# Leaving one branch of a nonlinearity out of the common path, with a check at the end and a recomputation behind a branch

## The chip, the cores and the metric

The kernel runs on one core of a Trainium2 chip. The metric is the device time of one execution in microseconds (us); the kernel before has a median of 1015.11 us in three runs (1015.0 to 1015.22).

## The reference

Three parts follow one another. A linear attention over q, k and v of (4, 8, 576, 64) gives 2304 tokens of 512 numbers. A first layer with a nonlinearity of its own takes them through 2048 hidden columns. A second layer sends each token to two of eight experts.

```python
def _moe_ref(x, w_in, w_out) -> np.ndarray:
    h = x @ w_in
    g = h - np.tanh(h)
    return (g @ w_out).astype(np.float32)
...
    noisy_logits = logits + noise_scale * noise
    top2 = np.argpartition(-noisy_logits, 2, axis=1)[:, :2]
...
            h = np.maximum(x[mask] @ w1[e], 0.0)
            out[mask] += top2_w[mask, k, None] * (h @ w2[e])
```

w_in and w_out arrive as 64-bit floats, and the kernel decodes them on the chip from their two 32-bit halves. With the reference's inputs h is small: its largest magnitude is 0.017.

## The kernel before

All matrix products of the two layers are made of three products of split operands: each operand is the sum of a rounded high part and the rest, and high x high, high x rest and rest x high are added in PSUM (L814 to L816 for the first product of a layer, L874 to L876 for the second).

The work of both layers is a list of units, `seq`. A unit of the first layer is one block of 384 tokens (six blocks, 0 to 5) and one of 16 slices of 128 hidden columns: `l1` computes h into one of two PSUM banks, `nonlin` computes the negative of g, `split` makes its high part on ScalarE and its rest on GpSimd (L861), and `l2` multiplies it with w_out three units later (`LAG`). Blocks 0 and 1 run interleaved, since they need each decoded weight slice first; blocks 2 to 5 follow one after the other. While blocks 0 and 1 run, `decode` turns the 16 slices of w_in and w_out into split weights: three bit operations on VectorE (L712, L713, L717) for each half slice, a rounding on ScalarE (L722) and a subtraction on GpSimd (L724). The next slices are loaded in SP's queue (`raw_load`, tiles `stage` and `raw`), which waits for a free buffer; behind them in the same queue stand the fills of the buffer `xs` and of the output with zeros and the loads of q, k and v for later blocks.

`nonlin` has two branches for h. Where h squared is at most 0.09 (`HC` is 0.3), a polynomial in u = h*h is used: p = -u*h * ((sqrt(G_Q)*(u + G_A))**2 + G_B). Elsewhere tanh(h) - h is taken. Both are computed for every element:

```python
        a1 = A.activation(tu, h, AF.Square)
        a2 = A.activation(tt, h, AF.Tanh)
        a3 = A.activation(tq, tu, AF.Square, bias=qbias[:, 0:1], scale=math.sqrt(G_Q))
        a4 = A.activation(tm, tu, AF.Relu, bias=qbias[:, 1:2])
...
        v4 = V.copy_predicated(tp, tm.bitcast(U32), tt)
```

Four instructions run on ScalarE and four on VectorE: L839 (-u*h), L840 (tanh(h) - h), L845 (times the polynomial) and L846 (the choice). For a few units a table `KN` moves the work of L845 to GpSimd (L843). The bank of h is free for the next unit but one when its last reader, L840, is through.

After the first layer, `route_*` compute each token's two experts, `scatter` writes the tokens to areas of `xs`, one per expert, with 608 rows computed in any case, and the units of the second layer read them from there. `overflow_counts` counts the rows of each expert during the second layer. At the end, `overflow` holds a branch: an expert with more rows than 608 gets the rest computed there. In the profiled execution that branch is not taken.

The order of the instructions on each engine is set by a scheduler from priorities, `issue_after` marks and the offsets in `KN`; `hooks` tie the steps to units.

Of the kernel before, what the change touches and what calls it, by code (L numbers as in the profile page):

```python
# [375 lines left out]
def moe_kernel(ctx, tc, q, k, v, w_in, w_out, w_gate, w_noise, noise, w1, w2, out, xs):  # L376
# [150 lines left out]
    gap = cp.tile([P, GAPS], F32, name="gap")  # L527
    prow = cp.tile([P, 1], F32, name="prow")
# [163 lines left out]

    W = {}
# [126 lines left out]
    def nonlin(U):  # L820
# [10 lines left out]
        tt = sp.tile([P, n], F32, tag="t", bufs=8, name=f"t{U}")  # L831
        tm = sp.tile([P, n], F32, tag="t", bufs=8, name=f"m{U}")
# [129 lines left out]
    def route_slots(blk):  # L962
# [15 lines left out]
        if blk == NBLK - 1:  # L978
# [19 lines left out]
    def scatter(blk, t):  # L998
        xa, sl = XA[blk], SL[blk]
        for i in range(2):  # L1000
            G.memset(spacer, 0.0)
            st = G.indirect_dma_start(out=xs, out_offset=bass.IndirectOffsetOnAxis(ap=sl[:, i, t:t + 1], axis=0),
                                      in_=xa[:, t, :], in_offset=None)
            for o in last_scatter:
                tc.declare_no_dep(st.ins, o.ins, reason="every token has its own rows")
            last_scatter.append(st)

    tiles_x = cp.tile([P, E + 1], I32, name="tiles_x")
    pad_row = cp.tile([P, E], I32, name="pad_row")

    def overflow_counts():
# [4 lines left out]
        V.tensor_add(c[:, 0, 0:GAPS], c[:, 0, 0:GAPS], gap)  # L1016
        V.tensor_add(c[:, 1, :], c[:, 0, :], eoff[:, 0, :])
        V.tensor_scalar(pad_row, c[:, 1, :], prow, None, op0=OP.add)
        V.tensor_scalar(c[:, 2, :], c[:, 0, :], float(P - 1 - CAP), 0.0, op0=OP.add, op1=OP.max)
        V.tensor_copy(tiles_x[:, 0:E], c[:, 2, :])  # L1020
        V.tensor_scalar(tiles_x[:, 0:E], tiles_x[:, 0:E], 7, None, op0=OP.logical_shift_right)
# [4 lines left out]
    def overflow():  # L1026
# [3 lines left out]
        with tc.If(some > 0):  # L1030
# [3 lines left out]
            for e in range(E):  # L1034
# [7 lines left out]
                with tc.For_i(0, n, 1) as it:  # L1042
# [6 lines left out]
                    for c in range(NC):  # L1049
                        T.transpose(pt[:, c * P:(c + 1) * P], x[:, c * P:(c + 1) * P], ident)  # L1050
# [173 lines left out]
```

## Time and profile before

| | us |
|---|---|
| median of three runs | 1015.11 |
| the profiled execution | 1017.24 |
| its span, first to last instruction | 1015.4 |
| TensorE busy | 958.9 (94%) |
| VectorE busy | 627.2 (62%) |
| ScalarE busy | 455.8 (45%) |
| GpSimd busy | 285.5 (28%) |

The span is divided below into stretches: up to 48 us the attention of block 0 and the first loads, 48 to 178 us blocks 0 and 1 with the decode, 178 to 500 us the rest of the first layer up to the middle of block 5, 500 to 580 us the change to the second layer, then the experts, and from 1005.5 us the last scatter. In the profile PE is TensorE, DVE VectorE, ACT ScalarE, POOL GpSimd, SP the queue engine. A row of a wait names who waited, for whom, the sum in us, how often, and the longest. A row of a line gives the busy time and the mean length of one instruction in ns. Busy time is the union of the rows, so rows of one engine can add up to a little more.

### The profile page before, as it was taken

The numbers are of one execution on the slowest core, as the hardware profiler recorded it, in microseconds if no ns is written. First come the engines' busy times: TensorE is split into PE (matmuls) and PEld (weight loads), VectorE is DVE, ScalarE is ACT, GpSimd is POOL, SyncE is SP. The second block draws the span as 40 slices with busy tenths as digits, with TensorE's granted clock in tenths as the row PEclk, the third lists the DMA queues.
The fourth block names the chain that finished last, engine by engine and source line by source line (L and its number), as shares of the span: only waits on it lengthen the run. The fifth ranks groups of instructions, "written<-read, shape, count | busy, mean of one in ns | idle before, by whom it ended". The sixth has DMA issues, their size and how long they took to land.

```text
span 1015.4 us, 14696 instructions
## 1 busy us (share of the span) xinstructions
PE 958.9 (94%) x5311; PEld 844.0 (83%) x5311; DVE 627.2 (62%) x1339; ACT 455.8 (45%) x981; POOL 285.5 (28%) x278
## 2 busy tenths in 40 slices
PE   4988887999999999999989999999999999999996
PEld 2766676989888999999978888988889888888885
DVE  7999999876778856756774623635353534444221
ACT  2665564676556556566754312423232323333110
POOL 4555546422234242242241211111101011111102
PEclk9999999999999999999999999999999999999999
DMA  9935775111342010010350641845353645443203
GB/s 260 334 114 171 240 282 182 39 40 26 74 130 77 25 65 22 21 65 1 104 177 30 209 100 23 216 112 137 79 174 62 167 100 131 106 113 79 27 12 49
DMA packets 106962, 111.13 MB, mean 109 GB/s; under 512 B 28032, under 2 KB 79232, under 8 KB 106880
## 3 DMA queue, kind: packets, MB, share of 16 engines
q1 hardware_dynamic: 98496, 90.40, 28.8%
q0 software_dynamic: 8384, 19.70, 10.2%
q8 instruction: 44, 0.72, 0.3%
q14 instruction: 38, 0.31, 0.1%
HBM read 74.87 MB, written 35.21 MB: 108 GB/s over the span
## 4 chain that ended last, share of the span: by engine, by line
PE 74%; DVE 13%; DMA 5%; issue 4%; POOL 2%; ACT 1%; SPq 1%; DVEq 0%; POOLq 0%; ACTq 0%
PE y L876 11%; PE y L875 11%; PE y L874 11%; PE h L814 11%; PE h L816 11%; PE h L815 11%; DVE dec L713 2%; DMA stage<-in_moe_w_in 2%; DVE p L845 2%; PE xgt L782 1%; DVE p L846 1%; DVE dec L717 1%; PE lg L912 1%; DMA xg<-xs 1%; PE xp L688 1%
## 5 line engine op out<-in xcount | busy, mean ns | idle before, releaser
L876 PE MATMUL y<-w,g 128*128 128x512 f32 (+1 forms) x608 | 240.6, 396 | 0.2
L875 PE MATMUL y<-w,g 128*128 128x512 f32 (+1 forms) x608 | 240.4, 395 | 0.0
L874 PE MATMUL y<-w,g 128*128 128x512 f32 (+1 forms) x608 | 240.2, 395 | 0.0
L826 ACT ACTIVATE g<-h 128x352 fp32r<-128x352 f32 (+1 forms) x128 | 54.3, 424 | 315.2 <-PE y L876 307.4
L827 DVE SCALAR_TENSOR_TENSOR g<-h,g 128x352 fp32r<-128x352 f32 (+1 forms) x128 | 60.5, 472 | 217.7 <-ACT g L826 217.7
L861 POOL TENSOR_TENSOR g<-p,g 128x384 fp32r<-128x384 f32 x96 | 104.4, 1089 | 224.5 <-ACT g L860 79.9
L1075 POOL DMA_INDIRECT out<-yo,gm x40 | 62.8, 1569 | 364.6 <-DVE yo L1074 266.8
L814 PE MATMUL h<-xgT,w 128*128 128x352 f32 (+1 forms) x512 | 159.5, 311 | 0.6 <-DVE g L827 0.6
L814 PE MATMUL h<-xT,w 128*128 128x384 f32 x384 | 135.8, 355 | 24.3 <-DVE t L840 15.9
L815 PE MATMUL h<-xgT,w 128*128 128x352 f32 (+1 forms) x512 | 154.4, 302 | 1.2 <-DVE xgT L784 1.2
L816 PE MATMUL h<-xgT,w 128*128 128x352 f32 (+1 forms) x512 | 154.4, 302 | 0.0
L876 PEld LDWEIGHTS y<-w,g 128*128 128x128 f32 (+1 forms) x608 | 112.5, 185 | 30.0 <-POOL g L861 1.4
L816 PE MATMUL h<-xT,w 128*128 128x384 f32 x384 | 131.0, 341 | 0.5 <-POOL w L724 0.5
L815 PE MATMUL h<-xT,w 128*128 128x384 f32 x384 | 130.4, 340 | 1.0 <-DVE xT L691 1.0
L875 PEld LDWEIGHTS y<-w,g 128*128 128x128 f32 (+1 forms) x608 | 112.6, 185 | 19.0
L874 PEld LDWEIGHTS y<-w,g 128*128 128x128 f32 (+1 forms) x608 | 112.7, 185 | 17.7 <-ACT g L860 0.2
L814 PEld LDWEIGHTS h<-xT,w 128*128 128x128 f32 x384 | 73.1, 191 | 33.8 <-DVE t L840 19.7
L814 PEld LDWEIGHTS h<-xgT,w 128*128 128x128 f32 x512 | 96.5, 188 | 5.3 <-DVE g L827 1.2
L815 PEld LDWEIGHTS h<-xgT,w 128*128 128x128 f32 x512 | 96.7, 189 | 4.8 <-DVE xgT L784 1.6
L816 PEld LDWEIGHTS h<-xgT,w 128*128 128x128 f32 x512 | 96.4, 188 | 0.0
L839 DVE SCALAR_TENSOR_TENSOR p<-u,h 128x384 f32<-128x384 f32 x96 | 52.7, 549 | 58.7 <-ACT t L835 54.2
L744 DVE TENSOR_TENSOR w<-raw,w 128x512 fp32r<-128x512 f32 x128 | 84.3, 694 | 6.5 <-ACT w L742 5.6
(181 smaller groups left out, 1465.1 us busy)
## 6 DMA issues: line engine op xcount, KB each, us to landing
raw<-in_moe_w SPq DMA_DIRECT2D x128, 256.0 KB, 3.2
xs<-pad SPq DMA_DIRECT2D x16, 528.0 KB, 6.6
xg<-xs SPq DMA_DIRECT2D x16, 528.0 KB, 4.3
stage<-in_moe_w_in SPq DMA_DIRECT2D x13, 512.0 KB, 10.0
stage<-in_moe_w_out SPq DMA_DIRECT2D x13, 512.0 KB, 9.7
out<-pad SPq DMA_DIRECT2D x4, 1280.0 KB, 8.9
qr<-in_q SPq DMA_DIRECT2D x20, 192.0 KB, 3.5
k<-in_k SPq DMA_DIRECT2D x8, 256.0 KB, 5.7
```

Source lines behind the costliest of these rows:

```text
L744: V.tensor_sub(wt[:, 2 * i + 1, :], s, wt[:, 2 * i, :].bitcast(F32))
L814: T.matmul(h, wh, x[:, 0, c, :], start=(c == 0), stop=False)
L815: T.matmul(h, wh, x[:, 1, c, :], start=False, stop=False)
L816: T.matmul(h, wl, x[:, 0, c, :], start=False, stop=(c == NC - 1))
L826: LA[U] = A.activation(g[:, 0, :], h, AF.Relu)
L827: LV[U] = V.scalar_tensor_tensor(g[:, 1, :], h, 0.0, g[:, 0, :].bitcast(F32), op0=OP.max, op1=OP.subtract)
L839: v1 = V.scalar_tensor_tensor(tp, tu, -1.0, h, op0=OP.mult, op1=OP.mult)
L861: G.tensor_sub(g[:, 1, :], tp, g[:, 0, :].bitcast(F32))
L874: T.matmul(y, gh, w[:, 2, :], start=first, stop=False)
L875: T.matmul(y, gh, w[:, 3, :], start=False, stop=False)
L876: T.matmul(y, gl, w[:, 2, :], start=False, stop=last)
L1075: o = G.indirect_dma_start(out=out, out_offset=bass.IndirectOffsetOnAxis(ap=g.bitcast(U32)[0:m, t, 1:2], axis=0), in_=yo[0:m], in_offset=N ...
```

## The change

`nonlin` keeps the polynomial branch alone. Tanh, the mask, the subtraction L840 and the choice L846 go; the square of h also adds up its values per partition into a column of a new tile `usum`, one column per unit. All units compute the last product on VectorE, and GpSimd's L843 goes. For the check at the end the largest of the 96 sums of each partition is compared with 0.09, and a matmul with ones counts the partitions above. The sum over 384 tokens is at least its largest member, so no single square above 0.09 passes unseen. The final branch, now `rare`, is taken if an expert overflows or if the count is above zero; in the second case `general` clears the output, loads and decodes the weights again, computes the first layer with both branches and routes and computes all experts anew. For that the split inputs of the six blocks are saved to a new buffer `xd` in HBM (`x_save`), 1536 KB each.

```diff
-        a1 = A.activation(tu, h, AF.Square)
-        a2 = A.activation(tt, h, AF.Tanh)
-        a3 = A.activation(tq, tu, AF.Square, bias=qbias[:, 0:1], scale=math.sqrt(G_Q))
-        a4 = A.activation(tm, tu, AF.Relu, bias=qbias[:, 1:2])
-        ACTS[U] = (a1, a2, a3, a4)
+        a1 = A.activation(tu, h, AF.Square, accum_out=usum[:, U:U + 1])
+        a2 = A.activation(tq, tu, AF.Square, bias=qbias[:, 0:1], scale=math.sqrt(G_Q))
+        ACTS[U] = (a1, a1, a2, a2)
         v1 = V.scalar_tensor_tensor(tp, tu, -1.0, h, op0=OP.mult, op1=OP.mult)
-        v3 = V.tensor_sub(tt, tt, h)
-        if K('tqp%d' % U, 0):
-            A.activation(tq, tq, AF.Relu, bias=qbias[:, 2:3])
-            v2 = PS[U] = G.tensor_mul(tp, tp, tq)
-        else:
-            v2 = V.scalar_tensor_tensor(tp, tq, G_B, tp, op0=OP.add, op1=OP.mult)
-        v4 = V.copy_predicated(tp, tm.bitcast(U32), tt)
-        VS[U] = (v1, v3, v3 if U in PS else v2, v4)
-        LA[U], LV[U] = a4, v4
+        v2 = V.scalar_tensor_tensor(tp, tq, G_B, tp, op0=OP.add, op1=OP.mult)
+        VS[U] = (v1, v1, v2, v2)
+        LA[U], LV[U] = a2, v2
...
+    def x_save(blk):
+        Y.dma_start(xd[blk], XT[blk].bitcast(F32).rearrange("p a c s -> p (a c s)"))
...
+        V.tensor_reduce(over, usum, axis=AX, op=OP.max)
+        V.tensor_scalar(over_b, over, HC * HC, None, op0=OP.is_gt)
+        T.matmul(pp[:, E:E + 1], ones_b, over_b, start=True, stop=True)
+        V.tensor_copy(tiles_x[:, E + 1:E + 2], pp[:, E:E + 1])
         V.tensor_reduce(c[:, 1, 0:1], c[:, 0, :], axis=AX, op=OP.add)
+        V.tensor_add(c[:, 1, 0:1], c[:, 1, 0:1], pp[:, E:E + 1])
         V.tensor_copy(tiles_x[:, E:E + 1], c[:, 1, 0:1])
...
+    def rare():
+        some = nc.values_load(tiles_x[0:1, E:E + 1], min_val=0, max_val=E * (AREA // P) + P,
                               skip_runtime_bounds_check_because=why)
         with tc.If(some > 0):
...
+            expert_rows(CAP)
+            big = nc.values_load(tiles_x[0:1, E + 1:E + 2], min_val=0, max_val=P,
+                                 skip_runtime_bounds_check_because=why)
+            with tc.If(big > 0):
+                general()
...
+    for blk in range(NBLK):
+        at(pos["m", 0, 5] + blk if blk < 2 else pos["m", blk, 2], x_save, blk)
```

The line numbers shift: L814 to L816 become L818 to L820, L839 keeps its number, L845 becomes L840, L712, L713 and L717 become L716, L717 and L721, and the maximum of q, L654, becomes L655.

VectorE at the decode of column 10, before: u, q, t, m and p are the tiles of `nonlin`, `dec` those of a decode; `stage_466` is column 9, `stage_683` column 10.

```order
L839 SCALAR_TENSOR_TENSOR p_1077<-u_1073,h_1059 128x384
L717 SCALAR_TENSOR_TENSOR dec_1_1052<-stage_466,dec_1_1052 128x512
L840 TENSOR_TENSOR t_1075<-t_1075,h_1059 128x384
L845 SCALAR_TENSOR_TENSOR p_1077<-q_1074,p_1077 128x384
L712 TENSOR_SCALAR dec_0_1098<-stage_683 128x512
L846 COPY_PREDICATED p_1077<-m_1076,t_1075 128x384
L713 SCALAR_TENSOR_TENSOR dec_0_1098<-stage_683,dec_0_1098 128x512
L712 TENSOR_SCALAR dec_1_1142<-stage_683 128x512
L717 SCALAR_TENSOR_TENSOR dec_0_1098<-stage_683,dec_0_1098 128x512
L839 SCALAR_TENSOR_TENSOR p_1122<-u_1118,h_1104 128x384
L840 TENSOR_TENSOR t_1120<-t_1120,h_1104 128x384
```

And the same place after; `stage_662` is column 10, `stage_742` column 11.

```order
L839 SCALAR_TENSOR_TENSOR p_1006<-u_1004,h_990 128x384
L716 TENSOR_SCALAR dec_0_1023<-stage_662 128x512
L840 SCALAR_TENSOR_TENSOR p_1006<-q_1005,p_1006 128x384
L717 SCALAR_TENSOR_TENSOR dec_0_1023<-stage_662,dec_0_1023 128x512
L716 TENSOR_SCALAR dec_1_1061<-stage_662 128x512
L721 SCALAR_TENSOR_TENSOR dec_0_1023<-stage_662,dec_0_1023 128x512
L717 SCALAR_TENSOR_TENSOR dec_1_1061<-stage_662,dec_1_1061 128x512
L716 TENSOR_SCALAR dec_0_1132<-stage_742 128x512
L721 SCALAR_TENSOR_TENSOR dec_1_1061<-stage_662,dec_1_1061 128x512
L717 SCALAR_TENSOR_TENSOR dec_0_1132<-stage_742,dec_0_1132 128x512
L839 SCALAR_TENSOR_TENSOR p_1045<-u_1043,h_1029 128x384
L721 SCALAR_TENSOR_TENSOR dec_0_1132<-stage_742,dec_0_1132 128x512
```

Of each unit two instructions are left; the last one that reads h is L839, which stands ahead of the decode instruction behind which L840 stood.

SP's queue from the load of column 10 on, before: `stage_683`, `stage_775` and `stage_823` are columns 10 to 12, `qr` is the q of block 2.

```order
L409 DMA stage_683<-in_moe_w_in 128x4x256
L411 DMA stage_683<-in_moe_w_out 128x1024
L484 DMA qr_0_1464<-in_q 64x4x192 x2
L559 DMA xs<-pad 256x1x528
L561 DMA xs<-pad 96x528
L409 DMA stage_775<-in_moe_w_in 128x4x256
L411 DMA stage_775<-in_moe_w_out 128x1024
L559 DMA xs<-pad 256x1x528 x2
L409 DMA stage_823<-in_moe_w_in 128x4x256
L411 DMA stage_823<-in_moe_w_out 128x1024
```

SP's queue after, the saves of blocks 0 and 1 (`xd`) with the loads of columns 10 to 12 around them:

```order
L411 DMA stage_662<-in_moe_w_out 128x1024
L695 DMA xd<-xT_419 128x3072
L409 DMA stage_742<-in_moe_w_in 128x4x256
L411 DMA stage_742<-in_moe_w_out 128x1024
L695 DMA xd<-xT_525 128x3072
L409 DMA stage_784<-in_moe_w_in 128x4x256
```

Each save now stands between two weight loads. Eight rows further down in SP's queue after, the q of block 2 (`qr`) with the first fills of `xs`:

```order
L484 DMA qr_0_1341<-in_q 64x4x192 x2
L560 DMA xs<-pad 256x1x528
L562 DMA xs<-pad 96x528
L560 DMA xs<-pad 256x1x528 x2
L562 DMA xs<-pad 96x528
L560 DMA xs<-pad 256x1x528 x2
L484 DMA qr_1_1344<-in_q 64x4x192 x2
```

All weight loads now stand ahead of the fills of `xs`, seven of which come between the two halves of q.

## Rows read from the trace of the kernel before

**Rows 1.** Busy us (instructions) of each engine, granted clock, DMA share, GB/s by stretch:

```profile
48.00:178.00 130.00, 104.31 (x494) 87.09 (x493) 129.76 (x184) 74.66 (x153) 74.28 (x55) 0.99 0.60 201
178.00:500.00 322.00, 321.87 (x1757) 290.79 (x1757) 231.84 (x548) 199.88 (x429) 101.21 (x100) 1.00 0.18 53
500.00:580.00 80.00, 76.06 (x408) 66.55 (x407) 53.50 (x176) 41.11 (x89) 21.62 (x21) 0.98 0.37 124
580.00:1005.50 425.50, 424.94 (x2485) 375.62 (x2483) 170.23 (x361) 118.72 (x272) 61.30 (x40) 1.00 0.43 102
1005.50:1015.40 9.90, 0.00 (x1) 0.00 (x0) 0.79 (x2) 0.00 (x0) 3.11 (x2) 0.75 0.44 58
```

**Rows 2.** TensorE's waits from 48 to 178 us, the longest in total:

```profile
PE h L814 <- DVE t L840: 15.9, 12, 3.2
```

**Rows 3.** Instructions in order of time around 164 us: start, length, what:

```profile
163.43 1.26 POOL L724 TENSOR_TENSOR w<-dec,w 128x512 fp32r<-128x512 f32 x1 [1.29 <-ACT w L722]
163.68 1.56 DVE L717 SCALAR_TENSOR_TENSOR dec<-stage,dec 128x512 uint32<-128x512 uint32 x1
165.16 0.54 DVE L840 TENSOR_TENSOR t<-t,h 128x384 f32<-128x384 f32 x1
...
165.76 0.45 PE L814 MATMUL h<-xT,w 128*128 128x384 f32 x1 [2.66 <-DVE t L840]
```

**Rows 4.** VectorE by line, 48 to 178 us: busy us, mean ns, idle before:

```profile
L717 DVE SCALAR_TENSOR_TENSOR dec<-stage,dec 128x512 uint32<-128x512 uint32 x25 | 26.2, 1056 | 0.0
L845 DVE SCALAR_TENSOR_TENSOR p<-q,p 128x384 f32<-128x384 f32 x21 | 22.2, 1057 | 0.0
L713 DVE SCALAR_TENSOR_TENSOR dec<-stage,dec 128x512 uint32<-128x512 uint32 x26 | 21.9, 854 | 0.0
L712 DVE TENSOR_SCALAR dec<-stage 128x512 uint32<-128x512 uint32 x26 | 18.5, 723 | 0.0
L846 DVE COPY_PREDICATED p<-m,t 128x384 f32<-128x384 uint32 x22 | 17.7, 805 | 0.2
L840 DVE TENSOR_TENSOR t<-t,h 128x384 f32<-128x384 f32 x23 | 12.5, 543 | 0.0
```

**Rows 5.** GpSimd by line, 48 to 178 us, three of its groups:

```profile
L724 POOL TENSOR_TENSOR w<-dec,w 128x512 fp32r<-128x512 f32 x27 | 38.9, 1449 | 28.9 <-ACT w L722 28.8
L861 POOL TENSOR_TENSOR g<-p,g 128x384 fp32r<-128x384 f32 x22 | 28.0, 1271 | 21.7 <-issue 13.3 <-ACT g L860 5.0 <-ACT g L858 3.4
...
L843 POOL TENSOR_TENSOR p<-p,q 128x384 f32<-128x384 f32 x2 | 2.8, 1392 | 2.0 <-DVE p L839 2.0
```

**Rows 6.** Single VectorE lines, 48 to 178 us: shortest/median/longest ns, first and last:

```profile
L712 DVE TENSOR_SCALAR dec<-stage x26: 399/420/2792, 48.1 to 171.2; 128x512 uint32<-128x512 uint32 x26
...
L713 DVE SCALAR_TENSOR_TENSOR dec<-stage,dec x26: 665/680/1770, 51.2 to 172.9; 128x512 uint32<-128x512 uint32 x26
...
L717 DVE SCALAR_TENSOR_TENSOR dec<-stage,dec x25: 664/1033/1779, 52.4 to 173.8; 128x512 uint32<-128x512 uint32 x25
...
L845 DVE SCALAR_TENSOR_TENSOR p<-q,p x21: 544/984/2473, 54.5 to 177.5; 128x384 f32<-128x384 f32 x21
...
L846 DVE COPY_PREDICATED p<-m,t x22: 582/598/1521, 55.6 to 172.4; 128x384 f32<-128x384 uint32 x22
```

**Rows 7.** One ScalarE line of the router, its shortest kind:

```profile
L951 ACT ACTIVATE rw<-rw x6: 205/205/206, 266.8 to 566.2; 128x3 f32<-128x3 f32 x6
```

**Rows 8.** The page's DMA issues: KB each, median us from issue to landing:

```profile
out<-pad SPq DMA_DIRECT2D x4, 1280.0 KB, 8.9
```

**Rows 9.** SP's queue in order of time, the load of column 10:

```profile
79.72 0.37 SPq L409 DMA_DIRECT2D stage<-in_moe_w_in  x1
```

**Rows 10.** VectorE in order of time, the first decode of column 10:

```profile
121.85 1.52 DVE L712 TENSOR_SCALAR dec<-stage 128x512 uint32<-128x512 uint32 x1
```

**Rows 11.** The matmul of the count of rows, one line:

```profile
L1013 PE MATMUL cnt<-msum,ones_b x1: 180/180/180, 599.9 to 599.9; 128*128 128x8 bf16 x1
```

**Rows 12.** TensorE's waits from 500 to 580 us, the longest in total:

```profile
PE pos L971 <- DVE mm L957: 1.5, 1, 1.5
```

More of the change, by code (lines that the diff above doesn't have):

```diff
@@ L375, in moe_kernel @@
 @with_exitstack
-def moe_kernel(ctx, tc, q, k, v, w_in, w_out, w_gate, w_noise, noise, w1, w2, out, xs):
+def moe_kernel(ctx, tc, q, k, v, w_in, w_out, w_gate, w_noise, noise, w1, w2, out, xs, xd):
     nc = tc.nc
@@ L527, in moe_kernel @@
     gap = cp.tile([P, GAPS], F32, name="gap")
+    usum = cp.tile([P, NBLK * NF1], F32, name="usum")
     prow = cp.tile([P, 1], F32, name="prow")
@@ new lines, in general @@
+    def general():
+        dst = out.rearrange("(p n) d -> p n d", p=P)
+        n_out = (N + TRASH) // P
+        for n0 in range(0, n_out, 5):
+            n1 = min(n_out, n0 + 5)
+            Y.dma_start(dst[:, n0:n1, :], pad[:, None, 0:DM].to_broadcast([P, n1 - n0, DM]))
+        V.memset(msum, 0.0)
+        for c in range(NF1):
+            for which in range(2):
+                t = sp.tile([P, 1024], U32, tag="raw", bufs=3, name=f"graw{c}_{which}")
+                RAW[c, which] = t
+                if which == 0:
+                    Y.dma_start(t.rearrange("p (c f) -> p c f", c=NC), w_in_u[:, :, c * 256:(c + 1) * 256])
+                else:
+                    Y.dma_start(t, w_out_u[c * P:(c + 1) * P, :])
+                decode(c, which)
+        for blk in range(NBLK):
+            n = BLOCKS[blk][2]
+            rows = n * P
+            x = sp.tile([P, 2, NC, rows], F32R, tag="xT", bufs=2, name=f"gx{blk}")
+            xr = sp.tile([P, 2, NC, rows], F32, tag="xT", bufs=2, name=f"gxr{blk}")
+            Y.dma_start(xr.rearrange("p a c s -> p (a c s)"), xd[blk])
+            A.activation(x, xr, AF.Copy)
+            YP["m", blk] = [bank("y", 3, f"gy{blk}_{t}") for t in range(n)]
+            for f in range(NF1):
+                w = W[f]
+                h = bank("h", 2, f"gh{blk}_{f}")[:, 0:rows]
+                for c in range(NC):
+                    wh, wl = w[:, 0, c * P:(c + 1) * P], w[:, 1, c * P:(c + 1) * P]
+                    T.matmul(h, wh, x[:, 0, c, :], start=(c == 0), stop=False)
+                    T.matmul(h, wh, x[:, 1, c, :], start=False, stop=False)
+                    T.matmul(h, wl, x[:, 0, c, :], start=False, stop=(c == NC - 1))
+                tu, tq, tt, tm, tp = [sp.tile([P, rows], F32, tag="t", bufs=8, name=f"g{z}{blk}_{f}") for z in "uqtmp"]
+                A.activation(tu, h, AF.Square)
+                A.activation(tt, h, AF.Tanh)
+                A.activation(tq, tu, AF.Square, bias=qbias[:, 0:1], scale=math.sqrt(G_Q))
+                A.activation(tm, tu, AF.Relu, bias=qbias[:, 1:2])
+                V.scalar_tensor_tensor(tp, tu, -1.0, h, op0=OP.mult, op1=OP.mult)
+                V.tensor_sub(tt, tt, h)
+                V.scalar_tensor_tensor(tp, tq, G_B, tp, op0=OP.add, op1=OP.mult)
+                V.copy_predicated(tp, tm.bitcast(U32), tt)
+                g = sp.tile([P, 2, rows], F32R, tag="gT", bufs=3, name=f"gg{blk}_{f}")
+                A.activation(g[:, 0, :], tp, AF.Copy)
+                G.tensor_sub(g[:, 1, :], tp, g[:, 0, :].bitcast(F32))
+                for t in range(n):
+                    gh, gl = g[:, 0, t * P:(t + 1) * P], g[:, 1, t * P:(t + 1) * P]
+                    y = YP["m", blk][t]
+                    T.matmul(y, gh, w[:, 2, :], start=(f == 0), stop=False)
+                    T.matmul(y, gh, w[:, 3, :], start=False, stop=False)
+                    T.matmul(y, gl, w[:, 2, :], start=False, stop=(f == NF1 - 1))
+            x2_evac(blk)
+            for t in range(n):
+                route_tr(blk, t)
+                route_logits(blk, t)
+            route_top(blk)
+            route_slots(blk, again=True)
+            for t in range(n):
+                scatter(blk, t, again=True)
+        tile_counts(0)
+        expert_rows(0)
```

117 lines of the change are left out of this document (62 added, 55 removed).

## The prediction

> **What bounds the kernel now.** I read the stretches first [rows 1]. From 178 to 500 us TensorE is busy 321.87 of 322 us, and from 580 us on it is as full, so nothing that another engine saves there can shorten the kernel; only what gives TensorE less to do could, and the change does not. From 48 to 178 us it is the other way round: VectorE is busy 129.76 of 130 us, TensorE only 104.31. This is the stretch in which blocks 0 and 1 of the first layer run while w_in and w_out are decoded on VectorE. The 25.7 us that TensorE stands there are the main thing to be won. Between 500 and 580 us it stands another 3.9 us.
>
> Next, who ends TensorE's waits in that stretch [rows 2]: the first matmul of a unit waits 12 times, 15.9 us in all, for the subtraction t = tanh(h) - h (L840), the last reader of the bank of h. One such place [rows 3]: the subtraction starts only at 165.16, because a decode instruction stands in front of it that took 1.56 us, and TensorE stood 2.66 us for it.
>
> Third, what fills VectorE [rows 4]: three decode lines (L712, L713, L717), and four instructions per unit: L839, L840, L845, L846. The change takes away L840 and L846. Fourth, why VectorE's rows are so long [rows 3 to 6]: L717 takes 0.664 us at its shortest and 1.56 us beside a GpSimd subtraction that began 0.25 us before it; the mean is 1.056 us. GpSimd is thus a partner in the bound, with 74.28 us of work in the stretch [rows 1].
>
> **The change part by part.**
>
> *Two instructions less per unit on VectorE.* Neighbouring rows overlap by 0.08 us (163.68 + 1.56 is 165.24, the next starts at 165.16 [rows 3]), so I take 0.08 us off each. L840: 23 x (0.543 - 0.08) = 10.6 us. L846: 22 x (0.805 - 0.08) = 16.0 us [rows 4]. Against that, the two units whose product ran on GpSimd (L843, [rows 5]) now run L845 on VectorE: 2 x (1.057 - 0.08) = 2.0 us. Net 24.6 us, and VectorE would need 129.8 - 24.6 = 105.2 us. But 22 x (0.805 - 0.582) = 4.9 us of L846 was waiting beside GpSimd [rows 4, 6], and GpSimd's work hardly shrinks (two L843, 2.8 us, [rows 5]); if those waits go over to the instructions that stay, it needs 110.1 us. I take the middle, 107.6 us, since both are as likely, and keep the ends.
>
> *The bank of h is released by another instruction.* Its last reader is now L839, which in the new order stands where it stood before, one to three instructions ahead of the old L840. That is part of the same 15.9 us [rows 2], not a second gain. What is late next is TensorE itself, 104.3 us, and the hand-over between the two. Two engines that both need about 105 us will not both be full. The nearest row for that is 500 to 580 us, where waits end now on one engine and now on another and TensorE is 95% busy [rows 1]. I take 107.6 / 0.95 = 113.3 us for the stretch, a gain of **16.7 us**. The ends are 104.3 us (TensorE without a gap: 25.7 us) and 110.1 / 0.95 = 115.9 us (14.1 us).
>
> *Two instructions less on ScalarE (Tanh, Relu)* cost and gain nothing by themselves: ScalarE is busy 74.66 of 130 us in the stretch and less elsewhere [rows 1]. What hides them is VectorE and TensorE; their going makes u, q and g arrive earlier.
>
> *The sum of squares.* The Square now also writes a sum per partition into a column of usum, 96 times. No accumulating instruction is in the trace. Bounds: nothing, if the sum is part of the same pass; or one smallest ScalarE instruction more each time, 0.205 us [rows 7], 24 x 0.205 = 4.9 us if every one in the stretch lay on the path. I take nothing, since ScalarE has 55 idle us there and one instruction of 0.2 us delays u only; 4.9 us stay in the range.
>
> *Six saves of the inputs of layer one.* Each writes 1536 KB. The output's fill writes 1280 KB in 8.9 us [rows 8], which scales to an estimate of 10.7 us. Blocks 0 and 1 are saved in the tight stretch, in SP's queue ahead of the weight loads of columns 11 and 12. What hides them is the lead of these loads: the load of column 10 is issued at 79.72 us [rows 9] and its first decode starts at 121.85 us [rows 10], 42 us later, four times one save. Cost nothing; without the cover 10.7 us each. The later four fall into stretches with a DMA share of 0.18 and 0.37 [rows 1]. In return the fills of xs, which stood between these loads, now stand behind them.
>
> *The check.* One reduction over 96 columns and one comparison, placed on VectorE long before they are used; one matmul of 128x1 like L1013, 0.18 us [rows 11]; two small instructions. In the second layer TensorE pays the matmul: 0.2 us. The final branch skips far more code than before; the skip runs in the last 9.9 us, in which the engines only wait for the last scatter [rows 1]. I take 0.2 us.
>
> *The end of the first layer.* At 510 us a position matmul waits 1.5 us for VectorE (L957, [rows 12]), which there runs the router's small steps between the four instructions of each unit. With two of these gone from each unit VectorE gets there some 1 us per unit sooner. I take **1.5 us**, between 0 and the 3.9 us of the stretch.
>
> *The sum.* 16.7 + 1.5 - 0.2 - 0.2 = 17.8 us. The profiled execution has a span of 1015.4 us and took 1017.24; it becomes 997.6 and 999.4. The median of the runs, 1015.11, stands 2.1 us below the profiled one, so 997.3: **997 us**.
>
> **A rule beside the rows.** The rows show VectorE held up by GpSimd, and most of a GpSimd instruction's length at that [rows 3, 6]. The Trainium skill, page "SBUF — State Buffer", section "Who interferes with whom", says that a VectorE instruction with two SBUF inputs and a GpSimd instruction that reads SBUF use one shared port pair, whoever comes first has it for the whole instruction and the other blocks; an instruction with an input in PSUM is free of it. By that rule taking L840 away (h is in PSUM) frees no port, only L846 does, and the gain would be that of the first rival below.
>
> **The rivals.**
>
> *GpSimd and VectorE together become the bound.* Take the VectorE instructions without a PSUM input at their shortest, from the counts of [rows 4, 6]: before, 25 x 0.664 + 26 x 0.665 + 26 x 0.399 + 21 x 0.544 + 22 x 0.582 = 68.5 us; after, without L846 and with two more L845, 56.8 us. Add GpSimd's 74.3 us, after 71.5 us [rows 1, 5]: 142.8 us before and 128.3 after. The first is more than the 130 us that the stretch lasted, so the trace does not bear out a full lock; it passed in 0.91 of the sum. 0.91 x 128.3 is 117 us, a gain of 13 us: 1001 us. For it: GpSimd's rows are long too, 1.449 us for L724 [rows 5]. Against: it leaves the PSUM instructions no place of their own.
>
> *TensorE reaches its own bound.* If VectorE falls clear below it, as after 178 us where it is 72% busy and TensorE waits for nothing [rows 1]: 25.7 + 1.5 - 0.4 gives 988 us.
>
> *A wait on the loads takes the place.* The second half of block 2's q now stands behind seven fills of xs in SP's queue, and its maximum stands on VectorE in front of a unit's L839. If it comes one 1280 KB fill late, 8.9 us [rows 8] less what other work hides, I take 6 us: 1003 us.
>
> *Slower.* The two saves lie on the path in full: 2 x 10.7 = 21.4 us in front of the loads of columns 11 and 12, and decode and TensorE stop for them. 997 + 21.4 is 1018 us. It decides when the lead of a weight load falls from 42 us to under some 20 us, a save and the load's own landing. Against it are [rows 9, 10] and the removal of the fills from between the loads.
>
> *The change does not do what it says.* If a sum of squares passes 0.09 the general path computes everything again, at least the 452 us of blocks 0 to 5 [rows 1], over 1460 us. With the reference's own inputs the largest sum over a block is 0.061; 1%.
>
> **How the numbers follow.** Forecast 52%, GpSimd and VectorE together 17%, TensorE's bound 14%, the loads 10%, slower 6%, recomputing 1%. The range reaches from the full gain of both stretches, 1015.1 - 25.7 - 3.9 = 986, to the loads' case with the sums' 4.9 us on the path, 1008. A difference of 0.2%, 2 us, is about what a measurement can tell. Faster 0.92, same 0.02, slower 0.06.
>
> **What would show it.** Right: TensorE's wait before L818 (the old L814) for the last reader of h falls from 15.9 us to under 5, VectorE stays over 90% busy until the decode ends, and the decode ends near 160 us instead of 178. The stretch after it is as full as now. Wrong: VectorE rows of the decode get longer than 1.06 us on average (the first rival); VectorE idle before L655 on a DMA (the loads); idle before L716 on a stage tile (the saves). The prediction falls if TensorE gains nothing while VectorE gets idle time.

## The result, and the profile after

The changed kernel takes **998.4 us** (median of 4 runs, 997.63 to 1001.56) against 1015.16 for the kernel before on the same chip (1015.0 to 1016.33): a ratio of 0.9838, 95% interval 0.9816 to 0.9861. That is 16.8 us less, where 18 were forecast (997 us). The profiled execution took 998.57 us with a span of 996.8 us, against 1015.4 us before.

First the stretches of the changed kernel, as in [rows 1]. Columns: stretch and its length, then busy us with the number of instructions of TensorE, its weight loads, VectorE, ScalarE and GpSimd, then granted clock, DMA share and GB/s.

```profile
48.00:161.00 113.00, 100.42 (x483) 87.19 (x483) 103.85 (x141) 52.67 (x122) 68.24 (x50) 0.97 0.69 239
161.00:482.00 321.00, 318.04 (x1743) 287.12 (x1741) 166.31 (x418) 153.74 (x357) 99.92 (x97) 1.00 0.25 78
482.00:562.00 80.00, 79.93 (x444) 71.54 (x445) 50.06 (x169) 38.52 (x88) 22.00 (x21) 1.00 0.40 134
562.00:987.00 425.00, 423.69 (x2481) 374.57 (x2479) 171.18 (x364) 118.67 (x272) 60.34 (x40) 1.00 0.42 102
```

The decode stretch is shorter, and VectorE is busy in 103.85 of its 113 us. The stretch after it is no longer quite full: TensorE stands 2.96 of 321 us, where it stood 0.13 of 322. The end of the first layer is full now, 79.93 of 80 us.

TensorE's longest wait between 48 and 178 us, in the place of [rows 2]: total us, times, longest.

```profile
PE h L818 <- DVE p L839: 7.2, 4, 2.8
```

It fell from 15.9 us in 12 places to 7.2 in 4. VectorE by line from 48 to 178 us, which here reaches 17 us past the decode, in the place of [rows 4] (with the new line numbers: L717 is here the second decode pass and L840 the product): busy us, mean ns, idle before and its releaser.

```profile
L840 DVE SCALAR_TENSOR_TENSOR p<-q,p 128x384 f32<-128x384 f32 x27 | 26.7, 988 | 3.9 <-ACT q L837 3.4
L717 DVE SCALAR_TENSOR_TENSOR dec<-stage,dec 128x512 uint32<-128x512 uint32 x26 | 23.6, 924 | 0.0
L721 DVE SCALAR_TENSOR_TENSOR dec<-stage,dec 128x512 uint32<-128x512 uint32 x25 | 21.4, 873 | 0.1
L716 DVE TENSOR_SCALAR dec<-stage 128x512 uint32<-128x512 uint32 x26 | 20.0, 786 | 0.0
L839 DVE SCALAR_TENSOR_TENSOR p<-u,h 128x384 f32<-128x384 f32 x27 | 14.8, 547 | 10.9 <-ACT u L836 10.9
```

VectorE now has idle time, nearly all of it before the two products, for u and q; up to 161 us it is 6.2 and 2.5 us. The rows of instructions that work in SBUF are still long beside their shortest ones (the second pass L717 0.676, the last L721 0.676, the product L840 0.546 us). Against the kernel before, the last pass got shorter (from 1.056 to 0.873 us), but the first and the second got longer (from 0.723 to 0.786 and from 0.854 to 0.924).

**Where the 18.6 us of the span went.** Each unit of the first layer has one Square of h on ScalarE, and each unit of the second one Relu. Their start times say how far the kernel is. The 33rd Square, for example, starts at 219.26 us before and at 204.56 after:

| start of | before, us | after, us | ahead by, us |
|---|---|---|---|
| Square 33 (decode over) | 219.26 | 204.56 | 14.7 |
| Square 49 | 313.95 | 301.83 | 12.1 |
| Square 81 | 464.01 | 451.74 | 12.3 |
| Relu 5 (second layer begun) | 566.33 | 547.41 | 18.9 |
| Relu 128, the last | 1001.34 | 982.20 | 19.1 |
| end of the span | 1015.4 | 996.8 | 18.6 |

So 14.7 us were gained beside the decode, 2.6 lost again by unit 49, 6.7 gained round the end of the first layer, and 0.5 lost at the end. These are differences between two single executions.

### The profile page after: what moved, and what is told of

Read it like the earlier page. It is cut to its first block, busy times and chain, and to the rows that moved or that the text cites. A ratio compares the mean times of both kernels' runs of the same rounds, so it can differ in the third digit from the quotient of the medians.

```text
span 996.8 us, 14406 instructions
## 1 busy us (share of the span) xinstructions
PE 953.2 (96%) x5312; PEld 844.0 (85%) x5312; DVE 531.7 (53%) x1158; ACT 384.6 (39%) x878; POOL 277.2 (28%) x271
## 3 DMA queue, kind: packets, MB, share of 16 engines
q0 software_dynamic: 8384, 19.70, 10.6%
## 4 chain that ended last, share of the span: by engine, by line
PE 78%; DVE 10%; DMA 4%; issue 3%; ACT 2%; POOL 1%; SPq 1%; ACTq 0%; DVEq 0%; POOLq 0%
PE y L870 12%; PE y L868 12%; PE y L869 12%; PE h L820 12%; PE h L818 12%; PE h L819 12%; DVE dec L717 2%; PE xgt L786 2%; DVE dec L716 1%; PE lg L906 1%; DVE p L840 1%; DVE dec L721 1%; PE xp L689 1%; DMA v<-in_v 1%; DMA head<-in_q 1%
## 5 line engine op out<-in xcount | busy, mean ns | idle before, releaser
L855 POOL TENSOR_TENSOR g<-p,g 128x384 fp32r<-128x384 f32 x96 | 104.5, 1090 | 228.6 <-ACT g L854 113.0
L818 PE MATMUL h<-xgT,w 128*128 128x352 f32 (+1 forms) x512 | 158.7, 310 | 0.7 <-DVE g L831 0.7
L820 PE MATMUL h<-xgT,w 128*128 128x352 f32 (+1 forms) x512 | 154.1, 301 | 0.0
L818 PE MATMUL h<-xT,w 128*128 128x384 f32 x384 | 134.0, 350 | 10.3 <-DVE p L839 7.2
L820 PE MATMUL h<-xT,w 128*128 128x384 f32 x384 | 130.9, 341 | 1.3 <-POOL w L728 1.3
L839 DVE SCALAR_TENSOR_TENSOR p<-u,h 128x384 f32<-128x384 f32 x96 | 52.8, 550 | 111.9 <-ACT u L836 106.5
L818 PEld LDWEIGHTS h<-xgT,w 128*128 128x128 f32 x512 | 96.2, 188 | 5.0 <-DVE g L831 1.1
L820 PEld LDWEIGHTS h<-xgT,w 128*128 128x128 f32 x512 | 96.2, 188 | 0.0
L818 PEld LDWEIGHTS h<-xT,w 128*128 128x128 f32 x384 | 72.7, 190 | 15.4 <-DVE p L839 6.2
```

Of the source, the lines that this page charges most:

```text
L818: T.matmul(h, wh, x[:, 0, c, :], start=(c == 0), stop=False)
L820: T.matmul(h, wl, x[:, 0, c, :], start=False, stop=(c == NC - 1))
L855: G.tensor_sub(g[:, 1, :], tp, g[:, 0, :].bitcast(F32))
```

## The experiments

The kernel before took 1015.2 to 1019.2 us (medians) on the chips of the five groups of runs, the first result among them, so the ratios are what to compare. "Time" below is ratio x 1015.2, to stand beside 998.8 (0.9838) for the changed kernel. Two ratios tell a difference only from some 3 us on, as their intervals say. "Ahead at Square 33" is the lead over the kernel before, as in the table, from one execution each: the five runs whose VectorE has the changed kernel's list there (the changed kernel, no_sums, no_saves, poly_only, q3_early) show 13.2 to 16.4 us, and the granted clock from 48 to 161 us lies between 0.94 (before_no846) and 1.00 (add_psum, low_on_v), so small differences in this column tell nothing.

| run | ratio, 95% interval | time, us | ahead at Square 33 |
|---|---|---|---|
| the changed kernel | 0.9838, 0.9816 to 0.9861 | 998.8 | 14.7 |
| no_sums | 0.9841, 0.9815 to 0.9868 | 999.1 | 15.0 |
| no_saves | 0.9824, 0.9798 to 0.9851 | 997.3 | 16.0 |
| poly_only | 0.9834, 0.9810 to 0.9858 | 998.3 | 16.4 |
| act_back | 0.9865, 0.9842 to 0.9889 | 1001.5 | 13.6 |
| add_psum | 0.9849, 0.9826 to 0.9871 | 999.9 | 12.1 |
| add_sbuf | 0.9966, 0.9949 to 0.9982 | 1011.7 | 2.7 |
| pool_light | 0.9674, 0.9655 to 0.9693 | 982.1 | 27.9 |
| q3_early | 0.9821, 0.9803 to 0.9838 | 997.0 | 13.2 |
| before_no840 | 0.9955, 0.9940 to 0.9969 | 1010.6 | 5.6 |
| before_no846 | 0.9867, 0.9845 to 0.9888 | 1001.7 | 15.5 |
| low_on_v | 0.9740, 0.9724 to 0.9755 | 988.8 | 24.3 |
| low_on_v_r5 | 0.9703, 0.9687 to 0.9720 | 985.0 | 23.7 |

### What the guard costs: no_sums, no_saves, poly_only

```diff
+    G.memset(usum, 0.0)
...
-        a1 = A.activation(tu, h, AF.Square, accum_out=usum[:, U:U + 1])
+        a1 = A.activation(tu, h, AF.Square)
```

> The changed kernel without the sums of squares: the first Square of each unit writes u alone, and the array of sums is filled with zeros once at the start, so the guard for large h is left without its numbers. The profile of the changed kernel shows the sum as a second ScalarE instruction of 0.193 us, 28 of them between 48 and 180 us. Theory that the sum costs nothing, as forecast (ScalarE has 60 idle us there): 997.5 to 999 us. Rival, the sum lies on the path of u, for which VectorE's first product waits 11.4 us in that stretch: 24 to 28 x 0.193 us = 4.6 to 5.4 us less, 993 to 994 us, and the wait of L839 on ScalarE's u falls by about as much.

The ratio is that of the changed kernel, 0.9841. The sum is a second ScalarE instruction, as the changed kernel's rows of that line show (shortest/median/longest ns, first and last start):

```profile
L836 ACT ACTIVATE u<-h x96: 471/492/508, 50.0 to 519.7; 128x384 f32<-128x384 f32 x96
L836 ACT ACTIVATION_READ_ACCUMULATOR u<-h x96: 190/194/226, 50.4 to 520.1; 128x1 f32 x96
```

Without it VectorE still waits 10.1 us for u in the stretch (10.9 with it). The theory that the sum costs nothing holds, within some 3 us; the rival's 5 us are not there.

```diff
-    for blk in range(NBLK):
-        at(pos["m", 0, 5] + blk if blk < 2 else pos["m", blk, 2], x_save, blk)
```

> The changed kernel without the six saves of the first layer's inputs; the branch for large h would then read nothing useful. Theory that the saves are hidden by the 42 us lead of the weight loads: 997.5 to 999 us, no change. Rival, the two saves in the tight stretch delay loads or slow the work beside them: 2 to 10 us less, 988 to 996 us.

0.9824, inside the changed kernel's interval. The six saves cost nothing that can be told: 1.4 us, with an uncertainty over twice that. The rival's 10 us are not there; its 2 us can't be ruled out.

```diff
-        V.tensor_reduce(over, usum, axis=AX, op=OP.max)
-        V.tensor_scalar(over_b, over, HC * HC, None, op0=OP.is_gt)
-        T.matmul(pp[:, E:E + 1], ones_b, over_b, start=True, stop=True)
...
-            with tc.If(big > 0):
-                general()
```

> The two instructions are taken off VectorE and ScalarE as in the change, and nothing is put in: no sums of squares, no saves, no comparison, no branch for large h. This tells the whole price of the guard. Theory of the forecast (sums and saves hidden, 0.2 us for the matmul, 0.2 us for the skipped branch): 997.5 to 998.5 us. Rival, the guard costs its instructions and transfers: 988 to 994 us; at 988 TensorE has reached its own bound in the stretch and the guard alone keeps the changed kernel from it.

This run has the two edits above as well. 0.9834: the whole guard costs nothing that can be told either. So it is not the guard that kept the decode stretch from TensorE's bound.

### Which of the two instructions it was: add_psum, add_sbuf, before_no840, before_no846

The forecast gave L840 10.6 us of the 24.6 and L846 16.0, as plain VectorE time. The next four runs price them singly, twice by putting one into the changed kernel, twice by taking one out of the kernel before.

```diff
         v1 = V.scalar_tensor_tensor(tp, tu, -1.0, h, op0=OP.mult, op1=OP.mult)
+        V.tensor_sub(tt, tu, h)
```

> The changed kernel with one VectorE instruction more per unit in the place of the old L840: a subtraction u - h, with u in SBUF and h in PSUM, whose result nobody uses. ScalarE keeps its short list. In the rows of before such a one took 0.543 us, so about 26 of them in the decode stretch are 26 x 0.46 = 12 us of VectorE. Theory that VectorE's time is the bound whatever the operands: 10 to 13 us over the changed kernel, 1008 to 1011 us, and TensorE's wait at L818 for the last reader of h grows by several us. Rival, only instructions with SBUF operands alone count, since these block GpSimd and are blocked by it: within 3 us of the changed kernel, 998 to 1001 us.

```diff
         v2 = V.scalar_tensor_tensor(tp, tq, G_B, tp, op0=OP.add, op1=OP.mult)
+        v2 = V.copy_predicated(tp, tu.bitcast(U32), tp)
```

> The changed kernel with one VectorE instruction more per unit in the place of the old L846: a predicated copy of p onto itself with u as the mask, all of it in SBUF, which leaves p as it was. In the rows of before it took 0.582 us at its shortest and 0.805 us on the mean, so 26 x 0.50 to 0.72 us is 13 to 19 us of VectorE in the decode stretch. Both theories give 11 to 16 us over the changed kernel, 1009 to 1014 us; the ratio to the run with the subtraction from PSUM tells them apart: about 1.1 to 1.5 if VectorE's time is the bound, 4 or more if only SBUF operands count.

The subtraction with an input in PSUM costs 1 us (0.9849), which can't be told from nothing, the copy in SBUF 13 (0.9966). Beside the decode the two cost 2.6 and 12.0 us of lead. The copy costs over 4 times the subtraction either way, as the theory of the SBUF operands had it. That the subtraction costs so little is what the forecast did not expect. Where its time went, from the run with the subtraction: the stretch by engine,

```profile
48.00:161.00 113.00, 97.09 (x479) 83.26 (x479) 107.59 (x159) 54.10 (x125) 67.05 (x49) 1.00 0.73 250
```

VectorE by line in it,

```profile
L842 DVE SCALAR_TENSOR_TENSOR p<-q,p 128x384 f32<-128x384 f32 x22 | 19.6, 891 | 0.2 <-ACT q L838 0.2
...
L721 DVE SCALAR_TENSOR_TENSOR dec<-stage,dec 128x512 uint32<-128x512 uint32 x24 | 18.0, 776 | 0.1
L841 DVE TENSOR_TENSOR t<-u,h 128x384 f32<-128x384 f32 x22 | 11.9, 542 | 0.0
```

and TensorE's longest wait from 48 to 170 us:

```profile
PE h L818 <- DVE t L841: 14.8, 9, 2.8
```

22 subtractions took 11.9 us. In the same 113 us VectorE's idle time went from 9.2 to 5.4 us, and of the rows behind two lines got shorter: in the changed kernel the second product (L840 there) took 1.047 us on the mean in this window and L721 0.873 us, here 0.891 and 0.776. A third got longer, L717 from 0.924 to 1.004 us. This fits with GpSimd getting on while VectorE reads PSUM, so that VectorE waits the less for it afterwards. That the subtraction is now what releases the bank of h is seen in the last row, 14.8 us in 9 places against 7.2 in 4.

```diff
-        v3 = V.tensor_sub(tt, tt, h)
+        v3 = v1
```

> The kernel before without L840 alone, the subtraction t = tanh(h) - h; where h is large the copy would take tanh(h) itself. All else stays, Tanh, Relu and the copy too. It takes 23 instructions of 0.543 us with h in PSUM off VectorE in the decode stretch, 10.6 us by the forecast's count, and TensorE's bank of h is then released by L839. Theory of the forecast (VectorE's time counts whatever the operands): 8 to 11 us less than the kernel before, 1004 to 1007 us for a kernel before of 1015. Theory that only the instructions in SBUF count, from the two runs with one instruction put back: 0 to 4 us less, 1011 to 1015 us.

```diff
-        v4 = V.copy_predicated(tp, tm.bitcast(U32), tt)
+        v4 = v3 if U in PS else v2
```

> The kernel before without L846 alone, the predicated copy, so that the branch of large h is computed and never used. It takes 22 instructions off VectorE that work in SBUF only, 0.805 us on the mean beside GpSimd. Theory of the forecast: 16.0 of the 24.6 us, so 10 to 11 us less than the kernel before, 1004 to 1005 us for a kernel before of 1015. Theory that only the instructions in SBUF count: 12 to 15 us less, 1000 to 1003 us, and what it leaves to the changed kernel is the ScalarE relief of about 3 us.

Taking L840 alone out of the kernel before brings 4.6 us (0.9955, 3.1 to 6.1 by its interval), L846 alone 13.5 (0.9867). That is 18.1 together, a little more than the 16.4 of the whole change by its ratio, and within the noise of it. The first figure lies between the two theories' ranges, nearer to the second. Without L840 VectorE stands idle in 10.1 of the 113 us from 48 us on, where it stood 0.2 before: most of what was taken off it came back as idle time. Why the subtraction is worth 4.6 us here and 1 in the changed kernel was not tested; that the kernel before has no idle time on VectorE to take it in is one reading. L846 carries three quarters of the gain.

### GpSimd's share: pool_light, low_on_v

```diff
-        with after(ap):
-            G.tensor_sub(wt[:, 2 * which + 1, :], t.bitcast(F32), wt[:, 2 * which, :].bitcast(F32))
+        A.activation(wt[:, 2 * which + 1, :], t.bitcast(F32), AF.Copy, scale=0.0)
```

> The changed kernel with GpSimd's subtraction of the decode (L728) replaced by a ScalarE pass that writes zeros, so that the low halves of w_in and w_out are missing from the result. It takes some 26 x 1.441 = 37 us off GpSimd's 68 us in the stretch and gives ScalarE about 26 x 0.6 = 16 us. VectorE's decode rows of the changed kernel are long beside their shortest: 0.873, 0.924 and 0.786 us against 0.664, 0.665 and 0.399 us, 22 us in all in the stretch. Theory that GpSimd's contention still sets part of VectorE's time: these rows fall to under 0.72, 0.72 and 0.55 us, and the kernel becomes 6 to 10 us faster, 988 to 992 us, where TensorE's bound stops it. Rival, the contention is a thing of VectorE's rows only and another wait takes over: 996 to 999 us.

Some 16 us faster than the changed kernel (0.9674), more than either theory gave, though VectorE lost no instruction. Its stretch by engine, and VectorE by line in it (L839 is here the product):

```profile
48.00:161.00 113.00, 109.39 (x550) 97.98 (x549) 92.05 (x151) 73.58 (x169) 35.86 (x29) 0.98 0.77 261
```

```profile
L839 DVE SCALAR_TENSOR_TENSOR p<-q,p 128x384 f32<-128x384 f32 x25 | 18.3, 731 | 8.3 <-ACT q L836 7.9
L721 DVE SCALAR_TENSOR_TENSOR dec<-stage,dec 128x512 uint32<-128x512 uint32 x25 | 18.1, 735 | 0.1
...
L716 DVE TENSOR_SCALAR dec<-stage 128x512 uint32<-128x512 uint32 x26 | 12.1, 478 | 0.5 <-PE xp L689 0.5
```

GpSimd has 35.86 us of work instead of 68.24, three of VectorE's four SBUF lines fell, and TensorE is busy 109.39 of 113 us. Of the expected lengths that of L717 was wrong; it stayed at 0.928 us. The lead of 27.9 us is more than the 25.7 us of idle time that the prediction took for TensorE's bound: TensorE's busy time from 48 us to Square 33 also fell, from 145.57 us in the kernel before to 139.51, so that bound was not the least.

```diff
+    PEND = []
...
+        if U is not None:
+            PEND.append((wt[:, 2 * which + 1, :], t.bitcast(F32), wt[:, 2 * which, :].bitcast(F32)))
+            return
         with after(ap):
             G.tensor_sub(wt[:, 2 * which + 1, :], t.bitcast(F32), wt[:, 2 * which, :].bitcast(F32))
...
             nonlin(U)
+        while PEND:
+            V.tensor_sub(*PEND.pop(0))
```

> The changed kernel with the decode's subtraction (L728) moved from GpSimd to VectorE for the columns that are decoded beside blocks 0 and 1, each placed behind the next unit's two products. GpSimd loses some 26 x 1.43 = 37 us of the stretch, VectorE gets 26 instructions more, which at the 0.664 us of its other pass over 512 elements are 17 us. Theory that the two engines share their time in SBUF: the shared sum falls by some 15 to 20 us, and the kernel becomes 4 to 10 us faster than the changed one, 988 to 994 us. Theory that VectorE's own time is the bound: 17 us more of it, less some 12 us of shorter rows, 1001 to 1006 us.

**990.13 us**, 0.974 of the kernel before: some 10 us faster than the changed kernel, with the same computation. VectorE was given more work and the kernel became faster. The stretch by engine, and VectorE by line in it (L718 is here the second decode pass, L844 the product, L1267 the moved subtraction):

```profile
48.00:161.00 113.00, 106.00 (x529) 92.64 (x528) 108.55 (x173) 59.01 (x137) 39.11 (x29) 1.00 0.77 260
```

```profile
L718 DVE SCALAR_TENSOR_TENSOR dec<-stage,dec 128x512 uint32<-128x512 uint32 x26 | 20.9, 820 | 0.0
...
L1267 DVE TENSOR_TENSOR w<-dec,w 128x512 fp32r<-128x512 f32 x25 | 18.1, 735 | 0.3 <-ACT w L727 0.2
L844 DVE SCALAR_TENSOR_TENSOR p<-q,p 128x384 f32<-128x384 f32 x25 | 16.8, 670 | 0.6 <-ACT q L841 0.3
```

25 subtractions took VectorE 18.1 us, where 26 had taken GpSimd 37.0; VectorE's second product fell from 1.047 to 0.670 us. That GpSimd's step was late for TensorE explains little of these two gains: TensorE waited only 1.3 us in all for L728's result in the changed kernel.

### ScalarE's relief: act_back

```diff
+        a3 = A.activation(tt, h, AF.Tanh)
         a2 = A.activation(tq, tu, AF.Square, bias=qbias[:, 0:1], scale=math.sqrt(G_Q))
-        ACTS[U] = (a1, a1, a2, a2)
+        a4 = A.activation(tm, tu, AF.Relu, bias=qbias[:, 1:2])
+        ACTS[U] = (a1, a3, a2, a4)
```

> The changed kernel with Tanh and Relu put back on ScalarE, where they stood before, their results unused. VectorE keeps its shorter list. Theory that only VectorE's relief counts: within 1 us of the changed kernel, 997.5 to 999.5 us. Rival, ScalarE's relief is part of the gain (u, q and g come earlier, and VectorE waits for u and q 15 us in the stretch): a half of the 17 us given back, 1003 to 1008 us.

0.9865, between the two, and its interval overlaps that of the changed kernel. Beside the decode it is 1.1 us behind the changed kernel, at the last Relu 5.1. The rival's half is not there, but some 3 us of the gain may be ScalarE's; it can't be settled from this.

### The new wait: q3_early, low_on_v_r5

In the stretch from 180 to 500 us the changed kernel has one wait of weight, which the kernel before does not have:

```profile
PE qt L676 <- ACT BD L644: 2.2, 1, 2.2
```

```diff
-    q_sched(3, pos["m", 2, 0] + 1, ...)
+    q_sched(3, pos["m", 2, 0] - 4, ...)
```

> The changed kernel with the load of q for block 3 issued five units earlier, ahead of the loads of k and v of the second batch. In the profile of the changed kernel TensorE waits 2.2 us at 275 us for BD of the second batch, a wait that the kernel before does not show, and VectorE waited 1.4 us for this q load just before. Theory that this load is the cause: 1.5 to 2.5 us off, 996 to 997 us, and no wait of L676 left. Rival, the chain through k, v and the router's steps on VectorE sets it: no change, 998 to 999 us, and the wait stays.

The wait stayed, at 2.5 us, and the ratio is that of the changed kernel within the noise (0.9821). The edit also missed its mark: the load that VectorE waited for at 270 us is block 4's, issued at 265.95 us in the changed kernel and at 265.26 us here. What stands in front of BD is to be read on VectorE (start, length), in the changed kernel:

```profile
276.86 0.15 DVE L634 TENSOR_SCALAR rs<-kv 128x1 f32<-128x1 f32 x1
276.97 0.18 DVE L933 SCALAR_TENSOR_TENSOR rt<-rt 128x24 f32<-128x24 f32 x1
...
278.69 0.14 DVE L944 TENSOR_TENSOR rw<-rt 128x3 f32<-128x3 f32 x1
278.75 0.15 DVE L634 TENSOR_SCALAR rs<-kv 128x1 f32<-128x1 f32 x1
...
278.93 0.17 DVE L640 RECIPROCAL rs<-rs 128x2 f32<-128x2 f32 x1
```

The two sums that BD needs stand 1.9 us apart, with the router's steps of block 1 between them. In the kernel before (L633 there) they start at 290.62 and 291.27 us, 0.65 us apart. The last run moved that router one unit on:

```diff
-        u = pos["m", 2, LAG + K('r1', 4) * blk] if blk < 2 else ...
+        u = pos["m", 2, LAG + 5 * blk] if blk < 2 else ...
```

> The run before (the decode's subtraction on VectorE) with the router of block 1 one unit later, so that on VectorE the sums of the last key pair of the second batch (rs, L634 and L640) stand ahead of the router's small steps and not among them. In the changed kernel TensorE waits 2.2 us at 277.6 us for BD, which waits for these sums; the load of q that was moved in another run did not touch it. Theory that the router's steps ahead of the sums are the cause: the wait falls under 0.5 us and 1.5 to 2.5 us go, a ratio to the kernel before of about 0.972 against 0.974. Rival, the sums are late for another reason: the wait stays near 2 us and the ratio at 0.974.

No wait of L676 is left; the longest in that stretch is now

```profile
PE kv L630 <- issue: 1.0, 1, 1.0
```

So the order of the router and the sums was the cause of that wait. The ratio fell to 0.9703, on another chip than the 0.9740, and the two intervals do not touch by a little; 3.7 us is more than the wait. In the profiled executions the lead at Square 49 rose from 20.2 to 23.0 us, yet at the last Relu it is 26.2 against 26.7 us: there it was given back round the end of the first layer, where this execution shows a granted clock of 0.96 from 482 to 562 us. The timed runs say faster, the one profile does not say by how much. It is the fastest version here that computes everything, 989.26 us on a chip on which the kernel before took 1019.23.

## Why the prediction was right, and where its steps were not

**The total** of 997 us against 998.4 is right because wrong sizes nearly cancel. The span was to fall by 17.8 us and fell by 18.6: the decode stretch was taken 2.0 us too high (16.7 against 14.7), all that comes later 2.8 us too low (1.1 against 3.9). The median fell by less, 16.8 us, since the profiled execution of before stood 2.1 us above its median and that of after 0.2.

**The bound.** That TensorE waits beside the decode for VectorE at the bank of h was read rightly, and both instructions off VectorE's list help. The step that failed is "Two instructions less per unit on VectorE": it counted each by its own length, as if VectorE's time alone set the stretch. VectorE's busy time did fall about as counted, from 129.76 us of 130 to 103.85 of 113, but 9.2 us of the 113 are now idle. L840, with h in PSUM, was given 10.6 of the 24.6 us; the runs give it 1 to 5 us, and L846 13.

**The rival that was set aside.** The first rival held that VectorE and GpSimd share time in SBUF, and it was put down with the words that 142.8 us of their work passed in 130 us. That sum took VectorE's rows at their shortest but GpSimd's at their measured length, which has GpSimd's own waiting for VectorE in it. GpSimd's shortest rows were there to be read in the kernel before (shortest/median/longest ns):

```profile
L724 POOL TENSOR_TENSOR w<-dec,w x27: 1262/1350/1742, 53.8 to 177.9; 128x512 fp32r<-128x512 f32 x27
...
L861 POOL TENSOR_TENSOR g<-p,g x22: 1001/1199/2294, 57.7 to 176.5; 128x384 fp32r<-128x384 f32 x22
```

With these, 27 x 1.262 + 22 x 1.001 + 2 x 1.329 (L843) + 2.76 and 2.61 (L666, the first from 48 us on) + 1.33 (L719) = 65.4 us. With VectorE's 68.5, which leaves out some 8 us of smaller rows, that is 133.9 us, and the stretch lasted 130. After the change it is 65.4 - 2.7 + 56.8 = 119.5 us, so 130 x 119.5 / 133.9 = 116.0 us: a gain of 14.0 us. The prediction's own figures for the rival gave 13. Both stand near the 14.7 us measured, and the forecast's 16.7 lies just above the 13.2 to 16.4 of the five runs with this list on VectorE; these sums alone would not decide between the two. The single instructions do, and the rows that follow.

**One engine at a time.** The changed kernel shows the sharing row by row. First VectorE from 85 us on, then GpSimd (start, length):

```profile
85.04 1.78 DVE L721 SCALAR_TENSOR_TENSOR dec<-stage,dec 128x512 uint32<-128x512 uint32 x1
86.74 0.54 DVE L839 SCALAR_TENSOR_TENSOR p<-u,h 128x384 f32<-128x384 f32 x1
87.21 1.04 DVE L717 SCALAR_TENSOR_TENSOR dec<-stage,dec 128x512 uint32<-128x512 uint32 x1
88.17 1.65 DVE L840 SCALAR_TENSOR_TENSOR p<-q,p 128x384 f32<-128x384 f32 x1
```

```profile
84.92 1.35 POOL L728 TENSOR_TENSOR w<-dec,w 128x512 fp32r<-128x512 f32 x1 [2.70 <-ACT w L726]
86.23 1.47 POOL L855 TENSOR_TENSOR g<-p,g 128x384 fp32r<-128x384 f32 x1
87.66 1.74 POOL L728 TENSOR_TENSOR w<-dec,w 128x512 fp32r<-128x512 f32 x1
```

Take each row's end less the shortest length of its line (L721 and L717 0.676, L840 0.546, L728 1.272, L855 1.007 us). L721 then really starts at 86.14, and GpSimd's L728 ended at 86.27. L855 starts at 86.69; L721 ended at 86.82. L717 starts at 87.57; L855 ended at 87.70. L728 starts at 88.13; L717 ended at 88.25. L840 starts at 89.27; L728 ended at 89.40. Five times one begins 0.12 to 0.13 us before the end of the other, near the 0.08 us by which neighbours on VectorE overlap: the two take turns. L839, with h in PSUM, takes its usual 0.54 us in the midst of L855.

So it is with every stretched row, and the kernel before shows it as well. From 48 to 178 us there, 46 rows of VectorE are at least 0.1 us longer than the shortest of their line, and from 48 to 161 us in the changed kernel 41. Each one's end less that shortest length lies 0.11 to 0.13 us before the end of a GpSimd row. Of the rows with an input in PSUM, 50 and 28, none is stretched by 0.1 us. If each row without such an input counts only with its shortest length before its end, VectorE or GpSimd is at work in 122 of the 130 us before and in 109 of 113 after, with low_on_v in 104 and with pool_light in 90 of 113: the two engines together were the bound in both kernels.

That is the rule of the Trainium skill, page "SBUF — State Buffer", section "Who interferes with whom", which the prediction weighed: the shared port pair goes to whoever comes first, for the whole instruction, and a VectorE instruction with at most one input in SBUF stays out of it unless it runs in a mode that uses both of its SBUF ports, which `tensor_scalar` can enter. These rows agree, those of L716, a `tensor_scalar`, with them, and so do the 1 us and 13 us of the two added instructions.

**The hand-over** was taken as a division by 0.95, for a stretch of 113.3 us; it lasted 115.3 (130 - 14.7). The term stood for TensorE and VectorE hindering each other, while the rows show VectorE and GpSimd doing so. VectorE's 9 idle us lie before the products, which wait for u and q of ScalarE; what they cost was not tested.

**The saves, the sums and the check** cost nothing that can be told from zero, to within some 3 us, as forecast.

**"The stretch after it is as full as now"** was wrong: a wait of 2.2 us on BD came up there, since the router's steps now stand between the two sums on VectorE. It was no case of the prediction. The rival that came nearest, a wait on the load of block 2's q, did not show in the changed kernel; in act_back and pool_light VectorE waits 2.0 and 1.1 us there.

**The end of the first layer** was given 1.5 us and brought 6.7. The row that the term went by, 1.5 us for L957 [rows 12], was one of three waits before, as TensorE's rows in order of time show (start, length, in brackets the wait):

```profile
510.60 0.19 PE L971 MATMUL pos<-mm,before 128*128 128x24 bf16 x1 [1.52 <-DVE mm L957]
531.60 1.36 PE L782 MATMUL xgt<-ident,xg 128*128 128x128 f32 x9 [1.04 <-DMA xg<-xs]
540.50 0.43 PE L815 MATMUL h<-xgT,w 128*128 128x352 f32 x1 [1.22 <-DVE xgT L784]
```

All three are gone, 3.8 us. The bound of 3.9 us from [rows 1] would have held these, but the prediction took the first alone. Another 1.7 us, by an estimate, is TensorE's clock, in the kernel before:

```profile
556.00:560.00 4.00, 4.00 (x18) 3.81 (x17) 2.72 (x9) 1.39 (x4) 0.00 (x0) 0.57 0.13 39
```

For 4 us the mean granted clock is 0.57, so nearly all of it at the lower level of 1.2 GHz, after a stretch from 532 us in which TensorE was busy 22.62 of 24 us; (1 - 0.57) x 4 = 1.7 us. The changed kernel has 1.00 there. That it is the vanished waits which spared it this dip was not tested: low_on_v_r5 shows 0.96 at this place with TensorE busy 79.59 of 80 us. The other 1.2 of the 6.7 us is not assigned.

**The signs.** The decode's last pass over a stage tile starts at 160.3 us instead of 173.8 [rows 6], and VectorE is 92% busy until then: as forecast. The wait for the bank of h fell to 7.2 us, not under 5. The sign for the first rival, decode rows longer than 1.06 us, could not tell it apart: no line passed 1.06 us (0.786 to 0.924 us; two lines got longer, one shorter), and yet the sharing was the bound, before and after.

## What to carry to other kernels

When two engines lengthen each other's rows, take a stretched row's end less the shortest length of its line: if that falls on the end of a row of the other engine, time after time, the two are one resource. Then add up both at their shortest lengths; a sum with one side's measured length has its waiting in it as well. In such a stretch the place of an instruction's operands decides what it is worth: here one with an input in PSUM was worth 1 to 5 us and one in SBUF 13, at nearly the same shortest length. Work can then be moved to the engine that looks full, if it is quicker there: 18 us on VectorE in place of 37 on GpSimd brought 10 us.

## What had not been expected of the hardware

The accumulating Square is two instructions on ScalarE, the second 0.194 us long and there 96 times, and its cost can't be found in the time. GpSimd's subtraction of 128x512 takes 1.27 us at its shortest, the same on VectorE 0.676. L716 has a single input, in SBUF, and yet its rows stretch beside GpSimd: 0.786 us on the mean, and 0.478 in pool_light with GpSimd's decode work gone, but still 0.749 in low_on_v (L717 there), where that work is gone too and GpSimd's other subtraction remains.
